# Making the y of two batches together in a fused scan and two MLPs kernel

## The chip, the core and the metric

The kernel runs on one core of a Trainium2 chip. The metric is the device time of one execution in microseconds: 617.73 as the median of three runs (617.5 to 618.22).

## What is computed

A gated linear scan (the mixer) is followed by two MLPs. For each batch b (4), head h (8) and chunk of the sequence, with cum the running sum of log a within the chunk:

```python
L = np.exp(cum[:, :, :, None] - cum[:, :, None, :]) * causal
M = np.einsum('bhin,bhjn->bhij', Cc, Bc) * L
y_intra = np.einsum('bhij,bhjd->bhid', M, xc)
y_inter = np.einsum('bhin,bhnd->bhid', Cc, state) * np.exp(cum)[:, :, :, None]
y[:, :, sl] = y_intra + y_inter
state = decay_full[:, :, None, None] * state + np.sum(Bx, axis=2)
...
x = softplus(x @ w_in) @ w_out        # first MLP, 3072 x 256 -> 2048 -> 256
x = gelu_sigmoid(x @ w2_in) @ w2_out  # second MLP, the same sizes
```

d = 32 columns of x per head, 16 states per head, 3072 = 4 x 768 positions.

## The kernel before

The sequence is cut into NC = 6 chunks of T = 128 positions. A *sub-chunk* s is one batch of one chunk: s = 4c + b, 24 in all. The main loop (line 510) has steps t; step t makes one slice of 128 hidden columns of an MLP for all 512 positions of a chunk (`g1`, six matmuls of 512 columns, line 359) and the second matrix product of the slice of two steps before (`g2`, lines 370 to 377: six matmuls with 512 columns; for t below 18 two matmuls in float32, each in two passes). 16 steps make a chunk. Steps 0 to 95 are the first MLP, 96 to 191 the second.

The mixer runs one chunk ahead of the first MLP, woven into steps 0 to 79: four steps for each sub-chunk, s = (c+1)*4 + (t mod 16)//4, with k = t mod 4 telling the part. Sub-chunks 0 to 3 are done before the loop. The order in each engine's queue is the order of the program text (the schedule is manual), so a function's place in the loop is its place in the queues:

- k = 0: `at_cb(s, 0)` on TensorE (C B^T for four heads, into the single PSUM bank `cb`); `at_small(s)`: two scans of dc on VectorE, cd = dc * ci and bs = B * last column of L on GpSimd.
- k = 1: `at_m(s, 0)` on VectorE (M = cb * L), which frees the bank for `at_cb(s, 1)`; `at_prep(s+1)` (tb, tc on ACT or VectorE, lb and rhs_bd on GpSimd).
- k = 2: `at_m(s, 1)`; `at_y(s)` and `at_u(s)` on TensorE.
- k = 3: `at_out(s)` (ACT copies y to xh, VectorE makes xl), `at_state(s)`, `at_scan(s+1)` (L of the next sub-chunk), `at_load(s+2)` (the loads, all on SP's queue).

`at_y(s)` has first the eight state products, on 32 rows and 32 columns each: head h of a group of four sits at rows 32h of state and cd and writes partitions 32h of y, so these use the four diagonal tiles of the array, twice (line 291). Then come eight products with M, all 128 rows and 32 columns (line 298), and `at_u` has eight more with 32 columns of data for the state's update (line 310). All are float32, two passes each.

In steps 0 to 13 the weights of the first MLP are put together from 64-bit words on VectorE, ACT and GpSimd as well (`w_sign`, `w_join_hi`, `w_join_lo`, `wi_split`; lines 103 to 142); in steps 14 to 28 w1o is split into a high and a low part on ACT and VectorE (`wo_split`).

Of the kernel before, what the change touches and what calls it, by code (L numbers as in the profile page):

```python
# [9 lines left out]
F32 = mybir.dt.float32  # L10
# [16 lines left out]
NT = NC * NF  # L27

PL_B, PL_C, PL_X, PL_BN, PL_W = 0, 128, 256, 512, 640
SP_B, SP_C, SP_X, SP_BN, SP_CI, SP_W = 0, 512, 1024, 1280, 1408, 1664  # L30

HI_SCALE = 2.0**-112


@with_exitstack
def mixer_two_mlps(ctx: ExitStack, tc: tile.TileContext, pack_p, pack_s, a_l, a_rows, consts, w1i, w1o, w2i, w2o, out):
    nc = tc.nc

    wts = ctx.enter_context(tc.tile_pool(name="wts", bufs=1))
# [111 lines left out]

    sub = {}

    def at_load(s):
        at_load_a(s)
        at_load_p(s)

    def at_load_a(s):
        c, b = divmod(s, NB)
        d = sub.setdefault(s, {})  # L160
        d["abz"] = at.tile([P, NH, T], F32, tag="abz", name=f"abz{s}")
        abz = d["abz"].rearrange("p h t -> p (h t)")
        r0 = s * NH
        if s < 2:
            for g in range(2 - s):
                o = slice(g * TB, (g + 1 + s) * TB)
                nc.sync.dma_start(out=abz[:, o], in_=a_l[s : s + 1, o].to_broadcast([P, (1 + s) * TB]))
        else:
            nc.sync.dma_start(
                out=abz, in_=scr_z[r0 : r0 + NH, :].rearrange("(o h) t -> o (h t)", o=1).to_broadcast([P, NH * T])  # L170
            )
        if c > 0:
            d["ad"] = at.tile([P, 2, T], F32, tag="ad", name=f"ad{s}")
            src = scr_a[r0 : r0 + NH, :].rearrange("(g h) t -> h g t", g=2)
            for h in range(4):
                nc.sync.dma_start(out=d["ad"][32 * h : 32 * h + 32], in_=src[h : h + 1].to_broadcast([32, 2, T]))

    def at_load_p(s):
        c, b = divmod(s, NB)
        d = sub.setdefault(s, {})  # L180
        if s < NB:
            pk = x2[:, (0, 1, 4, 5)[s]].rearrange("p k t -> p (k t)")
        else:
            pk = at.tile([P, SP_W], F32, tag="pk", name=f"pk{s}")
        if c == 0:
            nc.sync.dma_start(out=pk[:, 0:PL_W], in_=pack_p[s])
            d["B"], d["C"], d["x"], d["bn"] = pk[:, 0:PL_C], pk[:, PL_C:PL_X], pk[:, PL_X:PL_BN], pk[:, PL_BN:PL_W]
        else:
            nc.sync.dma_start(out=pk, in_=pack_s[s - NB])
            d["B"], d["C"], d["x"] = pk[:, 0:SP_C], pk[:, SP_C:SP_X], pk[:, SP_X:SP_BN]  # L190
            d["bn"], d["ci"] = pk[:, SP_BN:SP_CI], pk[:, SP_CI:SP_W]

    def at_prep(s):
        d = sub[s]
# [30 lines left out]
    def at_scan(s, half=0):  # L225
        d = sub[s]
        if "L" not in d:
            d["L"] = at.tile([P, NH, T], F32, tag="L", name=f"L{s}")
        h = slice(4 * half, 4 * half + 4) if s == 0 else slice(0, NH)
        if s < 2:  # L230
            clip(d["abz"][:, h], d["abz"][:, h])
            nc.vector.memset(d["abz"][:, h, 0:1], 0.0)
        nc.vector.tensor_tensor_scan(  # L233
            out=d["L"][:, h].rearrange("p h t -> p (h t)"), data0=d["abz"][:, h].rearrange("p h t -> p (h t)"),
            data1=eye8[:, h.start * T : h.stop * T], initial=0.0, op0=ALU.mult, op1=ALU.add,
        )

    def at_small(s):
        c, b = divmod(s, NB)
        d = sub[s]  # L240
        if c > 0:
            d["dc"] = at.tile([P, 2, T], F32, tag="dc", name=f"dc{s}")
            for g in range(2):
                nc.vector.tensor_tensor_scan(
                    out=d["dc"][:, g, :], data0=d["ad"][:, g, :], data1=zr, initial=1.0, op0=ALU.mult, op1=ALU.add
                )
            d["cd"] = at.tile([P, 2, T], F32, tag="cd", name=f"cd{s}")
            nc.gpsimd.tensor_tensor(
                out=d["cd"].rearrange("p g t -> p (g t)"), in0=d["dc"].rearrange("p g t -> p (g t)"), in1=d["ci"], op=ALU.mult
            )  # L250
        if c < NC - 1:
            nc.gpsimd.tensor_tensor(
                out=bs_t[s % 2][:, :, 0, :], in0=d["bn"].rearrange("p (h n) -> p h n", h=NH),
                in1=d["L"][:, :, T - 1 : T].to_broadcast([P, NH, N]), op=ALU.mult,
            )

    def at_cb(s, g):
# [14 lines left out]
    def at_m(s, g):  # L272
        d = sub[s]
        if s < NB:
            d["M", g] = hid.tile([P, TB], F32, tag="eg"[g], name=f"M{s}_{g}", bufs=2 + g).rearrange("p (h t) -> p h t", h=4)
        else:
            d["M", g] = at.tile([P, 4, T], F32, tag=f"M{g}", name=f"M{s}_{g}", bufs=1)
        nc.vector.tensor_mul(  # L278
            d["M", g].rearrange("p h t -> p (h t)"), d["cb", g], d["L"][:, 4 * g : 4 * g + 4, :].rearrange("p h t -> p (h t)")
        )  # L280

    def at_y(s):
        c, b = divmod(s, NB)
        d = sub[s]
        y = d["y"] = ps_y.tile([P, 512], F32, tag="y", name=f"y{s}")


        for g in range(2 if c > 0 else 0):
            for h in range(4):
                r = slice(32 * h, 32 * h + 32)  # L290
                nc.tensor.matmul(  # L291
                    y[r, g * T : g * T + T], state[b][r, g, :], d["cd"][r, g, :], start=(g == 0), stop=False,
                    skip_group_check=True,
                )
        for g in range(2):
            for h in range(4):
                x0 = g * P + h * D
                nc.tensor.matmul(  # L298
                    y[32 * h : 32 * h + 32, g * T : g * T + T], d["x"][:, x0 : x0 + D], d["M", g][:, h, :],
                    start=(c == 0), stop=True, skip_group_check=True,  # L300
                )

    def at_u(s):
        d = sub[s]
        y = d["y"]
        if s < NSUB - NB:
            for g in range(2):
                for h in range(4):
                    x0 = g * P + h * D
                    nc.tensor.matmul(  # L310
                        y[32 * h : 32 * h + 32, 256 + g * D : 256 + g * D + D],
                        bs_t[s % 2][:, 4 * g + h].rearrange("p s n -> p (s n)"), d["x"][:, x0 : x0 + D],
                        start=True, stop=True, skip_group_check=True,
                    )
# [29 lines left out]
    def at_pe(s, k):  # L344
        if k < 2:
            at_cb(s, k)
        elif k == 2:
            at_y(s)
            at_u(s)

    tt = {}
# [50 lines left out]
    with tc.manual_schedule():  # L402
# [107 lines left out]
        for t in range(2 * NT + 2):  # L510
# [25 lines left out]
            if mixing and late:  # L536
                at_pe(s, k)

            xl_of = at_out(s) if mixing and k == 3 else None
            if t < 2 * NT:  # L540
                d = tt[t]
                d["g"] = hid.tile([P, TB], F32, tag="g", name=f"g{t}")
# [13 lines left out]
            if t in (1, 3):  # L556
                at_state(2 + t // 2)
            if mixing:
                if k == 0:
                    at_small(s)  # L560
                elif k == 1:
                    if s + 1 < NSUB:
                        at_prep(s + 1)
                elif k == 3:
                    xl_of()
                    at_state(s)
                    if s + 1 < NSUB:
# [53 lines left out]
def _lay_out(x, a, B, C):  # L621
# [4 lines left out]
    xn = xc.transpose(0, 1, 3, 2, 4).reshape(NSUB, T, NH * D)  # L626
    bn = Bc.transpose(0, 1, 3, 2, 4).reshape(NSUB, T, NH * N)
    ci = Cc.reshape(NC, NB, 2, 4, T, N).transpose(0, 1, 3, 5, 2, 4)
    ci = np.broadcast_to(ci[:, :, :, None], (NC, NB, 4, 2, N, 2, T)).reshape(NSUB, P, 2 * T)

    def pairs(v):
        v = v[1:].reshape(NC - 1, NB, 4, 2, T, N).transpose(0, 1, 3, 5, 2, 4)
# [37 lines left out]
```

## Time and profile before

| | |
|---|---|
| median of three runs | 617.73 us (617.5 to 618.22) |
| the profiled execution: its own time | 617.93 us |
| its span, first to last instruction | 616.0 us |
| granted TensorE clock, mean | 0.993 |
| TensorE busy | 589.6 us, 96% of the span |
| VectorE busy | 378.0 us, 61% |
| ACT busy | 292.7 us, 48% |
| GpSimd busy | 158.2 us, 26% |

PE is TensorE's matmul, PEld its weight load, DVE VectorE, POOL GpSimd, SP the queue that issues the transfers. Times in the rows below are in microseconds from the span's start. The start-to-start distance of TensorE's rows tells how fast it goes; the durations overlap, since matmuls are pipelined.

### The profile page before, as it was taken

How to read it: one execution, taken by the hardware profiler on the slowest of the kernel's cores; microseconds unless marked ns; L12 is line 12 of the kernel's file. 1: busy time of each engine (PE TensorE's matmuls, PEld its weight loads, DVE VectorE, ACT ScalarE, POOL GpSimd, SP SyncE). 2: the span in 40 equal slices, each digit the busy share in tenths (PEclk: the TensorE clock that was granted, in tenths of full speed). 3: DMA queues.
4: the chain of work that ended last, by engine and by line, in shares of the span. 5: the costliest groups of instructions: out<-in, count | busy, mean ns of one | idle time of the engine just before them, and what ended most of it. 6: DMA issues, size and time to landing. Idle time of an engine off the chain costs nothing.

```text
span 616.0 us, 8790 instructions
## 1 busy us (share of the span) xinstructions
PE 589.6 (96%) x3392; PEld 461.2 (75%) x3392; DVE 378.0 (61%) x526; ACT 292.7 (48%) x501; POOL 158.2 (26%) x135
## 2 busy tenths in 40 slices
PE   4788889999999999999999999999999999999997
PEld 1355546888788888777788887888888888888885
DVE  5999996998877777787377699323323332332221
ACT  3344434454443444434455777544544554554543
POOL 2655444544454344453021233100000000000000
PEclk9889999999999999999999999999999999999999
DMA  6857653434334243343022241000000000000000
GB/s 209 279 194 234 214 196 106 147 100 138 102 99 147 107 141 99 99 139 118 2 69 77 94 145 61 35 1 0 35 0 1 34 2 0 35 1 0 35 0 34
DMA packets 24408, 54.39 MB, mean 88 GB/s; under 512 B 2832, under 2 KB 8368, under 8 KB 24368
## 3 DMA queue, kind: packets, MB, share of 16 engines
q1 hardware_dynamic: 24368, 53.85, 26.2%
q8 instruction: 26, 0.43, 0.3%
q14 instruction: 14, 0.11, 0.1%
HBM read 50.50 MB, written 3.34 MB: 87 GB/s over the span
## 4 chain that ended last, share of the span: by engine, by line
PE 81%; DVE 9%; DMA 3%; issue 3%; SPq 1%; POOL 1%; ACT 1%; DVEq 0%
PE h L359 37%; PE o L375 13%; PE o L377 12%; PE o L376 12%; PE y L298 2%; PE y L291 1%; DVE L L233 1%; PE cb L267 1%; DVE x L132 1%; DMA ac<-a_rows 1%; DMA pk<-pack_s 1%; DVE wt_1o L127 1%; DVE wt_1i L127 1%; PE o L373 1%; DMA wraw_1i<-w1i 1%
## 5 line engine op out<-in xcount | busy, mean ns | idle before, releaser
L76 DVE TENSOR_TENSOR gl<-g,gh 128x512 fp32r<-128x512 f32 x176 | 141.6, 806 | 170.1 <-ACT gh L382 170.0
L543 ACT ACTIVATE g<-h 128x512 f32<-128x512 f32 x192 | 114.8, 598 | 253.5 <-PE h L359 248.2
L382 ACT ACTIVATE gh<-g 128x512 fp32r<-128x512 f32 x176 | 111.3, 632 | 5.6
L359 PE MATMUL h<-xh,w1ih 128*128 128x512 f32 x192 | 78.6, 409 | 0.5 <-ACT xh L326 0.5
L359 PE MATMUL h<-xl,w1ih 128*128 128x512 f32 x192 | 76.2, 397 | 0.0
L377 PE MATMUL o<-gl,w2oh 128*128 128x512 f32 x192 | 74.8, 390 | 0.2 <-DVE gl L76 0.2
L359 PE MATMUL h<-x2h,w2ih 128*128 128x512 f32 x192 | 74.7, 389 | 0.0
L375 PE MATMUL o<-gh,w2ol 128*128 128x512 f32 x192 | 74.7, 389 | 0.0
L376 PE MATMUL o<-gh,w2oh 128*128 128x512 f32 x192 | 74.7, 389 | 0.0
L359 PE MATMUL h<-x2l,w2ih 128*128 128x512 f32 x192 | 74.7, 389 | 0.0
L79 POOL TENSOR_TENSOR rhs_bd<-tc,pk 64x512 fp32r<-64x512 f32 x40 | 65.1, 1628 | 1.5
L375 PE MATMUL o<-gh,w1ol 128*128 128x512 f32 x160 | 64.3, 402 | 0.0
L359 PE MATMUL h<-xh,w1il 128*128 128x512 f32 x192 | 60.2, 395 | 3.9 <-POOL w1il L79 3.9
L376 PE MATMUL o<-gh,w1oh 128*128 128x512 f32 x160 | 62.4, 390 | 0.0
L377 PE MATMUL o<-gl,w1oh 128*128 128x512 f32 x160 | 62.4, 390 | 0.0
L233 DVE TENSOR_TENSOR_SCAN L<-abz,eye 128x1024 f32<-128x1024 f32 (+1 forms) x25 | 61.8, 2474 | 0.2
L359 PE MATMUL h<-x2h,w2il 128*128 128x512 f32 x192 | 59.1, 389 | 0.0
L278 DVE TENSOR_TENSOR M<-cb,L 128x512 f32<-128x512 f32 x48 | 32.7, 686 | 28.3 <-PE cb L267 28.2
L359 PEld LDWEIGHTS h<-xh,w1il 128*128 128x128 f32 x192 | 36.2, 190 | 13.7 <-POOL w1il L79 5.6
L359 PEld LDWEIGHTS h<-xh,w1ih 128*128 128x128 f32 x192 | 36.6, 191 | 8.1 <-ACT xh L326 1.0
L377 PEld LDWEIGHTS o<-gl,w2oh 128*128 128x128 f32 x192 | 36.0, 188 | 8.2 <-DVE gl L76 0.7
L359 PEld LDWEIGHTS h<-xl,w1ih 128*128 128x128 f32 x192 | 36.6, 190 | 7.0 <-issue 1.0
(96 smaller groups left out, 753.0 us busy)
## 6 DMA issues: line engine op xcount, KB each, us to landing
pk<-pack_s SPq DMA_DIRECT2D x20, 832.0 KB, 4.6
abz<-scr_z SPq DMA_DIRECT2D x22, 512.0 KB, 3.7
wraw_1i<-w1i SPq DMA_DIRECT2D x8, 512.0 KB, 4.5
wraw_1o<-w1o SPq DMA_DIRECT2D x8, 512.0 KB, 3.6
wraw_2i<-w2i SPq DMA_DIRECT2D x8, 512.0 KB, 3.7
wraw_2o<-w2o SPq DMA_DIRECT2D x8, 512.0 KB, 3.4
out<-ot SPq DMA_DIRECT2D x12, 256.0 KB, 2.0
ad<-scr_a SPq DMA_DIRECT2D x80, 32.0 KB, 2.5
```

The lines of the kernel that those rows point to most:

```text
L76: nc.vector.tensor_sub(o, x, y)
L79: nc.gpsimd.tensor_tensor(out=o, in0=x, in1=y, op=ALU.subtract)
L127: nc.vector.scalar_tensor_tensor(out=tu, in0=tu, scalar=3, in1=s, op0=ALU.logical_shift_left, op1=ALU.bitwise_or)
L233: nc.vector.tensor_tensor_scan(out=d["L"][:, h].rearrange("p h t -> p (h t)"), data0=d["abz"][:, h].rearrange("p h t -> p (h t)"), data1=e ...
L278: nc.vector.tensor_mul(d["M", g].rearrange("p h t -> p (h t)"), d["cb", g], d["L"][:, 4 * g : 4 * g + 4, :].rearrange("p h t -> p (h t)"))
L298: nc.tensor.matmul(y[32 * h : 32 * h + 32, g * T : g * T + T], d["x"][:, x0 : x0 + D], d["M", g][:, h, :], start=(c == 0), stop=True, skip ...
L359: nc.tensor.matmul(h, w[:, k, f], x[:, k, :], start=(n == 0), stop=(n == 5))
L375: nc.tensor.matmul(acc[c][j], wl[:, m, o], d["gh"], start=first, stop=False)
L376: nc.tensor.matmul(acc[c][j], wh[:, m, o], d["gh"], start=False, stop=False)
L377: nc.tensor.matmul(acc[c][j], wh[:, m, o], d["gl"], start=False, stop=last)
L382: nc.scalar.activation(d["gh"], d["g"], AF.Copy)
L543: nc.scalar.activation(d["g"], d["h"], AF.Softplus if t < NT else AF.Gelu_apprx_sigmoid)
```

## The change

`at_y` and `at_u` of an even and the following odd sub-chunk are issued together, at k = 2 of the odd one. The odd sub-chunk keeps its state, ad, dc, cd and ci turned by 32 partitions (`rows(s, h)`: head h at rows 32((h+1) mod 4)), and its u is written there; its y stays at partitions 32h. The 16 state products of the two alternate between the sub-chunks, so that eight consecutive products have eight different tiles, and the two y are in two PSUM banks. M is written over L instead of into a tile of its own, L has three buffers; because bs reads L's last column, `at_small` makes bs first, and stands ahead of `at_m(s, 0)` in step 0. x, bn and ci are a transfer of their own (px, three buffers), and pk keeps B and C. At k = 3 of an odd sub-chunk both xh are copied, both xl made, then the next L, then both states.

```diff
-SP_B, SP_C, SP_X, SP_BN, SP_CI, SP_W = 0, 512, 1024, 1280, 1408, 1664
+SP_B, SP_C, SP_W = 0, 512, 1024
+SX_X, SX_BN, SX_CI, SX_W = 0, 256, 384, 640
...
+    def rows(s, h):
+        r = 32 * ((h + s % 2) % 4)
+        return slice(r, r + 32)
...
-                nc.sync.dma_start(out=d["ad"][32 * h : 32 * h + 32], in_=src[h : h + 1].to_broadcast([32, 2, T]))
+                nc.sync.dma_start(out=d["ad"][rows(s, h)], in_=src[h : h + 1].to_broadcast([32, 2, T]))
...
+            pk = at.tile([P, SP_W], F32, tag="pk", name=f"pk{s}")
+            px = at.tile([P, SX_W], F32, tag="px", name=f"px{s}", bufs=3)
             nc.sync.dma_start(out=pk, in_=pack_s[s - NB])
-            d["B"], d["C"], d["x"] = pk[:, 0:SP_C], pk[:, SP_C:SP_X], pk[:, SP_X:SP_BN]
-            d["bn"], d["ci"] = pk[:, SP_BN:SP_CI], pk[:, SP_CI:SP_W]
+            nc.sync.dma_start(out=px, in_=pack_x[s - NB])
+            d["B"], d["C"] = pk[:, 0:SP_C], pk[:, SP_C:SP_W]
+            d["x"], d["bn"], d["ci"] = px[:, 0:SX_BN], px[:, SX_BN:SX_CI], px[:, SX_CI:SX_W]
...
-            d["L"] = at.tile([P, NH, T], F32, tag="L", name=f"L{s}")
+            d["L"] = at.tile([P, NH, T], F32, tag="L", name=f"L{s}", bufs=3)
...
     def at_small(s):
         c, b = divmod(s, NB)
         d = sub[s]
+        if c < NC - 1:
+            nc.gpsimd.tensor_tensor(
+                out=bs_t[s % 2][:, :, 0, :], in0=d["bn"].rearrange("p (h n) -> p h n", h=NH),
+                in1=d["L"][:, :, T - 1 : T].to_broadcast([P, NH, N]), op=ALU.mult,
+            )
         if c > 0:
             d["dc"] = at.tile([P, 2, T], F32, tag="dc", name=f"dc{s}")
...
-        if c < NC - 1:
-            nc.gpsimd.tensor_tensor(
-                out=bs_t[s % 2][:, :, 0, :], in0=d["bn"].rearrange("p (h n) -> p h n", h=NH),
-                in1=d["L"][:, :, T - 1 : T].to_broadcast([P, NH, N]), op=ALU.mult,
-            )
...
-            d["M", g] = at.tile([P, 4, T], F32, tag=f"M{g}", name=f"M{s}_{g}", bufs=1)
+            d["M", g] = d["L"][:, 4 * g : 4 * g + 4, :]
...
+    def at_y(*ss):
+        for s in ss:
+            sub[s]["y"] = ps_y.tile([P, 512], F32, tag="y", name=f"y{s}")
+
+
+        for g in range(2 if ss[0] >= NB else 0):
             for h in range(4):
...
+                for s in ss:
+                    d, r = sub[s], rows(s, h)
+                    nc.tensor.matmul(
+                        d["y"][32 * h : 32 * h + 32, g * T : g * T + T], state[s % NB][r, g, :], d["cd"][r, g, :],
+                        start=(g == 0), stop=False, skip_group_check=True,
+                    )
+        for s in ss:
+            d = sub[s]
+            for g in range(2):
+                for h in range(4):
+                    x0 = g * P + h * D
+                    nc.tensor.matmul(
+                        d["y"][32 * h : 32 * h + 32, g * T : g * T + T], d["x"][:, x0 : x0 + D], d["M", g][:, h, :],
+                        start=(s < NB), stop=True, skip_group_check=True,
+                    )
...
-        elif k == 2:
-            at_y(s)
+        elif k == 2 and s % 2:
+            at_y(s - 1, s)
+            at_u(s - 1)
             at_u(s)
...
-            xl_of = at_out(s) if mixing and k == 3 else None
+            xl_of = [at_out(i) for i in (s - 1, s)] if mixing and k == 3 and s % 2 else []
...
             if t == 0:
+                at_small(s)
                 at_m(s, 0)
...
-                if k == 0:
+                if k == 0 and t > 0:
                     at_small(s)
...
-                    xl_of()
-                    at_state(s)
+                    for f in xl_of:
+                        f()
                     if s + 1 < NSUB:
                         at_scan(s + 1)
+                    for i in (s - 1, s) if s % 2 else ():
+                        at_state(i)
```

The host's layout follows: ci of odd batches is rolled by one group of 32 partitions, and pack_s is cut into pack_s and pack_x.

## Rows read from the trace of the kernel before

**Rows 1.** The page: shares of the engines, and the chain by engine.

```profile
PE 589.6 (96%) x3392; PEld 461.2 (75%) x3392; DVE 378.0 (61%) x526; ACT 292.7 (48%) x501; POOL 158.2 (26%) x135
...
PE 81%; DVE 9%; DMA 3%; issue 3%; SPq 1%; POOL 1%; ACT 1%; DVEq 0%
```

**Rows 2.** Stages: stretch, length, each engine's busy time (instructions), granted clock, DMA.

```profile
28.83:96.31 67.48, 59.01 (x376) 35.39 (x377) 63.53 (x83) 28.20 (x49) 35.82 (x29) 0.96 0.62 209
110.37:149.15 38.78, 38.78 (x302) 31.30 (x300) 37.90 (x51) 19.06 (x34) 18.61 (x15) 1.00 0.35 118
149.15:303.87 154.72, 154.72 (x1138) 124.06 (x1136) 114.14 (x161) 64.82 (x112) 62.85 (x53) 1.00 0.33 109
```

**Rows 3.** TensorE's timeline, steps 58 to 60: start, length, instruction, count.

```profile
232.67 0.40 PE L359 MATMUL h<-xh,w1ih 128*128 128x512 f32 x1
...
234.16 0.64 PE L291 MATMUL y<-cd,st 32*32 32x128 f32 x16
234.73 0.64 PE L298 MATMUL y<-M,pk 128*32 128x128 f32 x16
235.19 0.31 PE L310 MATMUL y<-pk,bs 128*32 128x32 f32 x16
235.43 0.50 PE L375 MATMUL o<-gh,w1ol 128*128 128x512 f32 x1
235.76 0.40 PE L376 MATMUL o<-gh,w1oh 128*128 128x512 f32 x1
236.00 0.39 PE L377 MATMUL o<-gl,w1oh 128*128 128x512 f32 x1
...
236.92 0.39 PE L359 MATMUL h<-xh,w1ih 128*128 128x512 f32 x1
...
239.64 0.39 PE L359 MATMUL h<-xh,w1ih 128*128 128x512 f32 x1
```

**Rows 4.** TensorE's timeline, starts of steps 78 and 79.

```profile
297.01 0.40 PE L359 MATMUL h<-xh,w1ih 128*128 128x512 f32 x1
...
301.13 0.40 PE L359 MATMUL h<-xh,w1ih 128*128 128x512 f32 x1
```

**Rows 5.** Line 291 alone in step 78: PE, PEld busy (passes begun by then).

```profile
298.45:298.60 0.15, 0.11 (x4) 0.11 (x8) 1.00 0.00 0
...
298.45:298.80 0.35, 0.31 (x12) 0.31 (x16) 1.00 0.00 0
```

**Rows 6.** ACT's timeline in step 9; in brackets the idle time before.

```profile
72.38 0.72 ACT L199 ACTIVATE tb<-pk,cc 128x512 fp32r<-128x512 f32 x1 [0.90 <-DMA pk<-pack_s]
```

**Rows 7.** Timelines of GpSimd, VectorE and TensorE in steps 12 to 14.

```profile
86.47 1.09 POOL L248 TENSOR_TENSOR cd<-dc,pk 128x256 f32<-128x256 f32 x1 [7.22 <-DVE dc L244]
87.52 0.41 POOL L252 TENSOR_TENSOR bs<-pk,L 128x128 f32<-128x128 f32 x1
...
92.29 0.68 DVE L278 TENSOR_TENSOR M<-cb,L 128x512 f32<-128x512 f32 x1
...
93.03 0.43 PE L298 MATMUL y<-M,pk 128*32 128x128 f32 x8 [0.24 <-DVE M L278]
```

**Rows 8.** Timeline of steps 18 to 20: GpSimd and VectorE.

```profile
105.94 3.44 POOL L79 TENSOR_TENSOR rhs_bd<-tc,pk 64x512 fp32r<-64x512 f32 x2
...
106.46 1.77 DVE L76 TENSOR_TENSOR w1ol<-x,w1oh 128x512 fp32r<-128x512 f32 x1
...
109.86 0.41 DVE L76 TENSOR_TENSOR xl<-y,xh 128x256 fp32r<-128x256 f32 x1
...
110.50 2.28 DVE L233 TENSOR_TENSOR_SCAN L<-abz,eye 128x1024 f32<-128x1024 f32 x1
...
113.29 0.68 DVE L76 TENSOR_TENSOR w1ol<-x,w1oh 128x512 fp32r<-128x512 f32 x1
```

**Rows 9.** Timeline of step 21: M and the cb that takes its bank.

```profile
114.54 0.67 DVE L278 TENSOR_TENSOR M<-cb,L 128x512 f32<-128x512 f32 x1
...
116.10 0.40 PE L267 MATMUL cb<-rhs_bd,lb 128*128 128x256 f32 x2
```

More of the change, by code (lines that the diff above doesn't have):

```diff
@@ L29, with mixer_two_mlps @@
 PL_B, PL_C, PL_X, PL_BN, PL_W = 0, 128, 256, 512, 640
-SP_B, SP_C, SP_X, SP_BN, SP_CI, SP_W = 0, 512, 1024, 1280, 1408, 1664
+SP_B, SP_C, SP_W = 0, 512, 1024
+SX_X, SX_BN, SX_CI, SX_W = 0, 256, 384, 640
 HI_SCALE = 2.0**-112
 @with_exitstack
-def mixer_two_mlps(ctx: ExitStack, tc: tile.TileContext, pack_p, pack_s, a_l, a_rows, consts, w1i, w1o, w2i, w2o, out):
+def mixer_two_mlps(ctx: ExitStack, tc: tile.TileContext, pack_p, pack_s, pack_x, a_l, a_rows, consts, w1i, w1o, w2i, w2o, out):
     nc = tc.nc
@@ L180, in at_load_p @@
         d = sub.setdefault(s, {})
-        if s < NB:
+        if c == 0:
             pk = x2[:, (0, 1, 4, 5)[s]].rearrange("p k t -> p (k t)")
-        else:
-            pk = at.tile([P, SP_W], F32, tag="pk", name=f"pk{s}")
-        if c == 0:
             nc.sync.dma_start(out=pk[:, 0:PL_W], in_=pack_p[s])
@@ L280, in at_m @@
         )
[L282 to L288, printed above, removed]
-            for h in range(4):
[L290 to L301, printed above, removed]
+    def at_y(*ss):
+        for s in ss:
+            sub[s]["y"] = ps_y.tile([P, 512], F32, tag="y", name=f"y{s}")
+        for g in range(2 if ss[0] >= NB else 0):
+            for h in range(4):
+                for s in ss:
[13 more added lines that the diff above has]
+                    )
     def at_u(s):
         d = sub[s]
-        y = d["y"]
         if s < NSUB - NB:
@@ L310, in at_u @@
                     nc.tensor.matmul(
-                        y[32 * h : 32 * h + 32, 256 + g * D : 256 + g * D + D],
+                        d["y"][rows(s, h), 256 + g * D : 256 + g * D + D],
                         bs_t[s % 2][:, 4 * g + h].rearrange("p s n -> p (s n)"), d["x"][:, x0 : x0 + D],
@@ L628, in _lay_out @@
     ci = Cc.reshape(NC, NB, 2, 4, T, N).transpose(0, 1, 3, 5, 2, 4)
-    ci = np.broadcast_to(ci[:, :, :, None], (NC, NB, 4, 2, N, 2, T)).reshape(NSUB, P, 2 * T)
+    ci = np.broadcast_to(ci[:, :, :, None], (NC, NB, 4, 2, N, 2, T)).copy()
+    ci[:, 1::2] = np.roll(ci[:, 1::2], 1, axis=2)
+    ci = ci.reshape(NSUB, P, 2 * T)
     def pairs(v):
@@ L639, in _lay_out @@
     pack_p = np.concatenate([first(Bc), first(Cc), xn[:NB], bn[:NB]], axis=2)
-    pack_s = np.concatenate([pairs(Bc), pairs(Cc), xn[NB:], bn[NB:], ci[NB:]], axis=2)
+    pack_s = np.concatenate([pairs(Bc), pairs(Cc)], axis=2)
+    pack_x = np.concatenate([xn[NB:], bn[NB:], ci[NB:]], axis=2)
     a_l = a.reshape(NB, NH, NC, T).transpose(2, 0, 1, 3)
-    return pack_p, pack_s, a_l.reshape(NSUB, NH * T), a_l.reshape(NSUB * NH, T)
+    return pack_p, pack_s, pack_x, a_l.reshape(NSUB, NH * T), a_l.reshape(NSUB * NH, T)
 def _consts():
@@ L655 @@
     from concourse.bass_utils import run_bass_kernel_spmd
-    pack_p, pack_s, a_l, a_rows = _lay_out(x, a, B, C)
-    arrays = {"pack_p": pack_p, "pack_s": pack_s, "a_l": a_l, "a_rows": a_rows, "consts": _consts()}
+    pack_p, pack_s, pack_x, a_l, a_rows = _lay_out(x, a, B, C)
+    arrays = {"pack_p": pack_p, "pack_s": pack_s, "pack_x": pack_x, "a_l": a_l, "a_rows": a_rows, "consts": _consts()}
     arrays = {k: np.ascontiguousarray(v) for k, v in arrays.items()}
```

## The prediction

> **What bounds the kernel now.** I read the page first, for the engines' shares and the chain that ended last; then the stages, for where TensorE has idle time; then the timeline of one step that holds a y; then what ends the idle time of the first 16 steps. The reader is to see that TensorE is busy for 96% of the span and carries 81% of the chain that ended last [rows 1]. By stage: in the first 16 steps (28.83 to 96.31) TensorE is busy 59.0 of 67.5 us and VectorE 63.5, so VectorE and what feeds it set the pace there. From 110.37 on TensorE is busy in every microsecond up to 303.87 [rows 2]. There a microsecond taken from TensorE's queue is a microsecond of the kernel, as long as nothing else becomes late. VectorE is nearly full in one more place, 110.37 to 149.15 (steps 20 to 31), where it has 0.9 us of idle time in 38.8 [rows 2].
>
> **What a y costs on TensorE.** A step begins with its first L359. Step 58 (k = 2, with a y) runs from 232.67 to 236.92, 4.25 us; step 59 without one from 236.92 to 239.64, 2.72 [rows 3]. The y and u of one sub-chunk thus cost 1.52 us. In the last mixing chunk, without u, step 78 takes 301.13 - 297.01 = 4.12 us [rows 4], a cost of 1.40; so u is 0.12.
>
> The 1.52 splits up like this. A sub-chunk has 8 state products, each a matmul in two passes: 16 records. By 298.60 four passes have started, by 298.80 twelve [rows 5]: they go in rounds of four, one on each of the four tiles on the diagonal, about 0.11 us a round, four rounds, 0.44 us. The products with M also are 16 records of 128 columns on four tiles, and u starts 235.19 - 234.73 = 0.46 us after them [rows 3]: again 0.44. What is left, 1.52 - 0.44 - 0.44 - 0.12 = 0.52 us, is the price of changing the tile shape three times (128x128 to 32x32 to 128x32 to 128x128). It shows at each border: L298 starts 0.57 after L291 where four rounds are 0.44, and the first L375 after the y takes 0.33 to the next start where the next take 0.24 [rows 3].
>
> **The change on TensorE.** The eight sub-chunk pairs of steps 16 to 79 lie in the stretch that TensorE bounds. A pair before: 2 x 1.52 = 3.04 us. After: one set of shape changes, 0.52; 32 passes of state products on eight tiles, which I put at four rounds of eight, 0.44 + 0.03 (starts within a round are spread wider); products with M for two, 0.88; u for two, 0.24. Sum 2.11, a saving of 0.93. Without u: 2.80 - 1.87 = 0.93 as well. Eight pairs: 7.4 us. Half of the 0.93 is the shape changes (0.52), the other half the rounds (0.41).
>
> The rounds are the uncertain half. That four 32x32 tiles with different rows and columns run together is in the trace, and that four 128x32 tiles that share all rows and differ in columns do, too. Two tiles in the same columns at once is not: the even sub-chunk's product sits at rows 32h, the odd one's at rows 32(h+1), both end in columns 32h. The bounds are four rounds (eight at once) and eight rounds (four at once), 0.44 us apart for a pair. I take four, because the nearest rows, the products with M, show tiles that share all their rows running together at the full round of 0.11 us, and because the two y go to two banks. [...] No row of this trace has two row tiles in one column.
>
> **What moves on the other engines.** ACT copies two xh in the odd k = 3 step instead of one in each; ACT is busy less than half of these stages [rows 2], so nothing. VectorE's xl and state updates of the even sub-chunk (together 0.65 us, from xl's start to the scan's [rows 8]) move four steps later, and the state updates behind the scan. At a chunk's end two xl stand before the next g1 instead of one, but the y they need is issued in the step before, as it was, and one xl of 0.41 us [rows 8] is covered by the g2 of that step (six starts 0.24 apart). M written over L takes as many elements as before. It adds one wait: the write of M must come after GpSimd has read the last column of L for bs. That is why bs goes first in at_small. GpSimd stood idle 7.2 us before cd in step 12 [rows 7], so bs runs in that idle time; behind the waiting M stand gl and the next cb, which show no lateness as long as bs is done before M's own cb. Without that cover it would cost bs's 0.41 us [rows 7] per sub-chunk. pk as two transfers: 20 more issues on SP, in front of nothing but later loads, for buffers that come free a step or more ahead (px has three, since x of the even sub-chunk lives longer). Nothing for these after step 16.
>
> **Steps 0 to 15.** TensorE's saving is not on the path there. Four things are. (a) VectorE must reach M of sub-chunk 7 (92.29), and TensorE waits for it 0.24 us [rows 7]; xl and the state updates of sub-chunk 6 were before it and now come after: 0.65 us earlier. (b) in step 9 ACT stood 0.90 us idle until pk of sub-chunk 7 had landed [rows 6]; with B and C alone it is 512 of 832 KB, so part of the 0.90 should go, and all of it is the most. (c) In step 14 the pair is 2.11 - 1.52 = 0.59 us longer than the single y was, less the 0.24 of waiting that the even sub-chunk's products now fill: 0.35 lost. (d) In step 0 the two dc scans and bs now go ahead of M: M is later by them, and GpSimd's queue (cd, then w1il, for which TensorE waits in step 2) is earlier by the M and the join that it stood behind; I count the two as even, a few tenths either way. The bounds are a gain of 2.0 (a, all of b, and d at 0.4) and a loss of 0.6 (neither a nor b counts, c stays, d costs 0.3). I take a gain of 0.7: a, 0.4 of b, less c.
>
> **Steps 16 to 31.** VectorE and GpSimd get in each other's way: w1ol took 1.77 us behind a rhs_bd and 0.68 without [rows 8]. TensorE gets faster by 1.86 over the two pairs of steps 16 to 31; VectorE had 0.9 us idle in most of that stretch [rows 2]. The tightest place I found is step 21: M ended at 115.21, the cb that needs its bank started at 116.10 [rows 9], 0.9 us of room; TensorE will come 1.52 earlier (no y in step 18) and VectorE 0.65. That just fits. Bounds 0 and 1.86 - 0.9 = 1.0; I take 0.2.
>
> Sum: 7.4 + 0.7 - 0.2 = 7.9 us less than the profiled execution's 617.93, which is 0.2 above the median of 617.73: 609.8. Its own range: 7.4 + 2.0 gives 608.3, 7.4 - 0.6 - 1.0 gives 611.9.
>
> **Rivals.**
> 1. Four at a time: two tiles in the same columns do not run together, or the engine doesn't look far enough ahead in its queue. Eight rounds, the pair takes 0.52 + 0.88 + 0.88 + 0.24 = 2.52, saving 0.52; 8 x 0.52 + 0.5 = 4.7 us, 613.0. For it: no row shows more than four at once. Against: each tile has its own rows and bank here.
> 2. VectorE takes over in steps 16 to 31 and nothing is gained up to there: six pairs are left, 5.6 us, 612.1. For it: VectorE's 0.9 us of idle time in 38.8. Against: the room in [rows 9], and 114.1 of 154.7 us busy from 149.15 on [rows 2].
> 3. Slower: the passes go in program order. In the program the two passes of one product follow each other on one tile, so in strict order each product's second pass waits out the first, and the next product starts with it: 17 rounds, a pair of 0.52 + 1.87 + 0.88 + 0.24 = 3.51 us, 0.47 more than before, 8 x 0.47 - 0.5 = 3.3 us, 621.0. It decides from 12.7 rounds on (3.04 - 0.52 - 0.88 - 0.24 = 1.40, by 0.11). Against it: strict order would give nine rounds, 0.99 us, for the eight products of before, and they take 0.57 with the shape change; so passes of other tiles overtake a waiting one. Whether they overtake when seven wait instead of three, and across tiles of one column, no row shows. [...]
> 4. No change to speak of: a new wait (M for bs, or the odd y for its cd) costs what the pairs save, 0.93 us for each of the eight. The idle 7.2 us on GpSimd speaks against it.
>
> **How the numbers follow.** The forecast has 0.62, rival 1 0.18, rival 2 0.08, rival 3 0.07, rival 4 0.05. The time is the forecast's, 609.8. The range takes the forecast's own lower end, 608.2, and goes up past rivals 1 and 2 to 613.5; rivals 3 and 4 and some of rival 1's tail are left out. About 0.2% (1.2 us) is what a measurement of this kernel can tell from no change. Faster by more than that: 0.62 + 0.18 + 0.08, and a little of rival 4: 0.89; same 0.04; slower 0.07.
>
> **What the profile after would show.** Steps of k = 2: even ones at 2.72 us, odd ones at 4.83 (2.72 + 2.11); with rival 1 at 5.24, with rival 3 at 6.2. By 0.15 us after the first state product eight passes should have started, not four. L298 should start about 0.6 us after L291. Steps 0 to 15 should end near 95.6 instead of 96.31. No idle time on TensorE between 110 and 300; idle before cb, ended by M, would be rival 2; idle before M, ended by bs, rival 4. I would be wrong above all if tiles in one column exclude each other.

## The result, and the profile after

The changed kernel takes 610.31 us (609.87 to 610.39) where the kernel before took 617.62 on the same chip: a ratio of 0.9879 (95% interval in brackets: [0.9862, 0.9896]). The forecast was 609.8. The profiled execution took 610.23 us, its span is 608.5.

The page after, the rows that answer to [rows 1]; TensorE's busy time is 6.9 us less for the same number of instructions:

```profile
PE 582.7 (96%) x3392; PEld 457.7 (75%) x3392; DVE 381.7 (63%) x526; ACT 292.3 (48%) x501; POOL 158.8 (26%) x135
...
PE 79%; DVE 10%; DMA 4%; issue 2%; POOL 2%; ACT 1%; SPq 0%; DVEq 0%; ACTq 0%; POOLq 0%
```

The stages that answer to [rows 2] (steps 0 to 15, 20 to 31, 32 to the end of the mixing; columns as there):

```profile
28.66:95.62 66.96, 59.01 (x376) 34.70 (x377) 63.49 (x79) 27.93 (x49) 35.89 (x29) 0.94 0.64 218
108.17:147.12 38.95, 38.86 (x349) 31.54 (x348) 38.91 (x49) 19.22 (x35) 18.62 (x16) 1.00 0.38 118
147.12:296.64 149.52, 149.52 (x1137) 122.39 (x1136) 117.92 (x165) 64.60 (x112) 64.57 (x53) 1.00 0.35 113
```

In steps 20 to 31 VectorE now has 0.04 us of idle time (38.91 of 38.95) and TensorE 0.09; from 147.12 on TensorE is the bound, as before.

TensorE's timeline after. First the odd step with the pair (step 54) and the start of steps 55 and 56; then an even step without a y (58), with the cb ahead of it; then steps 78 and 79, the pair without u. These rows answer to [rows 3, 4]:

```profile
214.58 0.40 PE L369 MATMUL h<-xh,w1ih 128*128 128x512 f32 x1
...
216.06 0.67 PE L299 MATMUL y<-cd,st 32*32 32x128 f32 x32
216.66 1.08 PE L308 MATMUL y<-L,px 128*32 128x128 f32 x32
217.56 0.48 PE L319 MATMUL y<-px,bs 128*32 128x32 f32 x32
217.96 0.50 PE L385 MATMUL o<-gh,w1ol 128*128 128x512 f32 x1
...
219.46 0.39 PE L369 MATMUL h<-xh,w1ih 128*128 128x512 f32 x1
...
222.18 0.39 PE L369 MATMUL h<-xh,w1ih 128*128 128x512 f32 x1
...
227.91 0.40 PE L274 MATMUL cb<-rhs_bd,lb 128*128 128x256 f32 x2
228.14 0.40 PE L369 MATMUL h<-xh,w1ih 128*128 128x512 f32 x1
...
230.91 0.39 PE L369 MATMUL h<-xh,w1ih 128*128 128x512 f32 x1
...
289.34 0.40 PE L369 MATMUL h<-xh,w1ih 128*128 128x512 f32 x1
...
293.92 0.39 PE L369 MATMUL h<-xh,w1ih 128*128 128x512 f32 x1
```

Step 54 is 219.46 - 214.58 = 4.88 us, step 58 is 2.77; the two were 4.25 each [rows 3]. The 32 passes of state products take 0.60 us to the next line's start, hardly more than the 0.57 that 16 took before. The pair without u makes step 78 4.58 us long.

The state products' line alone in step 78 (PE and PEld busy, in brackets the passes begun by then); it answers to [rows 5]:

```profile
290.78:290.93 0.15, 0.11 (x8) 0.11 (x16) 1.00 0.00 0
...
290.78:291.13 0.35, 0.31 (x24) 0.31 (x32) 1.00 0.00 0
```

Eight passes have begun by 0.15 us and 24 by 0.35, where it was four and twelve: eight tiles run together, in rounds of the same 0.11 us.

The lengths of the stretches, worked out from the starts of their first L359 (L369 after), give the account:

| steps | before, us | after, us | difference | predicted |
|---|---|---|---|---|
| start of step 0 | 28.83 | 28.66 | -0.17 | 0 |
| 0 to 15 | 67.48 | 66.96 | -0.52 | -0.7 |
| 16 to 31 (two pairs) | 52.84 | 51.50 | -1.34 | -1.66 |
| 32 to 63 (four pairs) | 103.41 | 100.08 | -3.33 | -3.72 |
| 64 to 79 (two pairs, no u) | 51.31 | 49.44 | -1.87 | -1.86 |
| 80 to the end | 312.18 | 311.81 | -0.37 | 0 |
| span | 616.05 | 608.45 | -7.60 | -7.9 |

Two rows of it are not the change's. The start of step 0 lay anywhere from 27.6 to 29.1 in the twelve executions profiled, and steps 80 to the end, which the change does not touch, took 311.78 to 312.18. I could not attribute either. Kernels that differ by a few tenths are therefore compared below by their stretches, not by their totals.

From step 16 on, one step without a pair got longer by more than 0.03 us: step 21, 3.36 us instead of 3.01. The timelines of VectorE, TensorE and GpSimd after, in step 14 (which answers to [rows 7]) and in steps 20 and 21 (to [rows 9]); in brackets the idle time before and its releaser:

```profile
91.06 0.86 PE L308 MATMUL y<-L,px 128*32 128x128 f32 x24
91.43 0.68 DVE L285 TENSOR_TENSOR L<-cb,L 128x512 f32<-128x512 f32 x1
92.16 0.43 PE L308 MATMUL y<-L,px 128*32 128x128 f32 x8 [0.24 <-DVE L L285]
...
111.37 0.66 DVE L77 TENSOR_TENSOR gl<-g,gh 128x512 fp32r<-128x512 f32 x1
111.58 0.72 POOL L249 TENSOR_TENSOR bs<-px,L 128x128 f32<-128x128 f32 x1 [2.88 <-issue]
111.96 0.90 DVE L77 TENSOR_TENSOR w1ol<-x,w1oh 128x512 fp32r<-128x512 f32 x1
113.43 0.66 DVE L285 TENSOR_TENSOR L<-cb,L 128x512 f32<-128x512 f32 x1
114.14 0.30 PEld L274 LDWEIGHTS cb<-rhs_bd,lb 128*128 128x128 f32 x2 [0.51 <-DVE L L285]
```

TensorE's weight load for the second cb stands idle 0.51 us until M has freed the bank. In front of that M, w1ol and bs ran into each other: bs, begun while gl ran, took 0.72 us instead of the 0.41 of step 12 [rows 7], and w1ol 0.90 instead of 0.68 [rows 8].

### The profile page after: what moved, and what is told of

It reads as the page before. It is cut to its first block, busy times and chain, and to the rows that moved or that the text cites. A ratio compares the mean times of both kernels' runs of the same rounds, so it can differ in the third digit from the quotient of the medians.

```text
span 608.5 us, 8823 instructions
## 1 busy us (share of the span) xinstructions
PE 582.7 (96%) x3392; PEld 457.7 (75%) x3392; DVE 381.7 (63%) x526; ACT 292.3 (48%) x501; POOL 158.8 (26%) x135
## 3 DMA queue, kind: packets, MB, share of 16 engines
HBM read 50.50 MB, written 3.34 MB: 88 GB/s over the span
## 4 chain that ended last, share of the span: by engine, by line
PE 79%; DVE 10%; DMA 4%; issue 2%; POOL 2%; ACT 1%; SPq 0%; DVEq 0%; ACTq 0%; POOLq 0%
PE h L369 37%; PE o L385 12%; PE o L387 12%; PE o L386 12%; DVE L L240 2%; DMA ad<-scr_a 2%; PE y L308 1%; PE cb L274 1%; DMA ac<-a_rows 1%; POOL rhs_bd L80 1%; DVE gl L77 1%; PE o L383 1%; PE y L299 1%; DVE x L133 1%; DVE wt_1i L128 1%
## 5 line engine op out<-in xcount | busy, mean ns | idle before, releaser
L369 PE MATMUL h<-xh,w1ih 128*128 128x512 f32 x192 | 79.0, 411 | 0.5 <-ACT xh L335 0.5
L369 PE MATMUL h<-xl,w1ih 128*128 128x512 f32 x192 | 75.9, 395 | 0.0
L369 PE MATMUL h<-x2h,w2ih 128*128 128x512 f32 x192 | 74.7, 389 | 0.0
L369 PE MATMUL h<-x2l,w2ih 128*128 128x512 f32 x192 | 74.7, 389 | 0.0
L240 DVE TENSOR_TENSOR_SCAN L<-abz,eye 128x1024 f32<-128x1024 f32 (+1 forms) x25 | 64.4, 2575 | 0.2
L369 PE MATMUL h<-xh,w1il 128*128 128x512 f32 x192 | 60.3, 395 | 2.3 <-POOL w1il L80 2.3
L369 PE MATMUL h<-x2h,w2il 128*128 128x512 f32 x192 | 59.1, 389 | 0.0
L369 PEld LDWEIGHTS h<-xh,w1il 128*128 128x128 f32 x192 | 35.9, 189 | 11.9 <-POOL w1il L80 4.1
L369 PEld LDWEIGHTS h<-xh,w1ih 128*128 128x128 f32 x192 | 36.8, 191 | 8.4 <-ACT xh L335 1.2
L369 PEld LDWEIGHTS h<-xl,w1ih 128*128 128x128 f32 x192 | 36.5, 190 | 7.5 <-issue 1.4
L386 PEld LDWEIGHTS o<-gh,w2oh 128*128 128x128 f32 x192 | 36.0, 188 | 7.5
```

The lines of the kernel that those rows point to most:

```text
L240: nc.vector.tensor_tensor_scan(out=d["L"][:, h].rearrange("p h t -> p (h t)"), data0=d["abz"][:, h].rearrange("p h t -> p (h t)"), data1=e ...
L369: nc.tensor.matmul(h, w[:, k, f], x[:, k, :], start=(n == 0), stop=(n == 5))
L386: nc.tensor.matmul(acc[c][j], wh[:, m, o], d["gh"], start=False, stop=False)
```

## The experiments

Each is the changed kernel with the edit shown.

**The odd sub-chunk on the same tiles as the even one.** The pair stays, the turn by 32 partitions goes (on the host the roll of ci goes with it), so sixteen products share four tiles.

```diff
     def rows(s, h):
-        r = 32 * ((h + s % 2) % 4)
+        r = 32 * h
```

> The pair as changed, but the odd sub-chunk is not turned: its state products use the same four diagonal tiles as the even one's. My theory (half of a pair's gain is that eight passes go at once, half is the shape changes shared): the state products of a pair take eight rounds instead of four, 0.44 us more for each of the eight pairs of steps 16 to 79, odd k = 2 steps of 5.32 us (4.88 before that edit) and 5.02 without u; 3.5 us more than the change, about 613.8. Rival (the gain is all shape changes, the rounds are hidden behind something else): no difference, 610.3.

Measured: 613.85 us (613.4 to 613.98), ratio 0.9939 [0.9925, 0.9954]. The state products' line alone, and TensorE's timeline of step 54:

```profile
217.73:217.88 0.15, 0.11 (x4) 0.11 (x8) 1.00 0.70 137
217.73:218.08 0.35, 0.31 (x12) 0.31 (x16) 1.00 0.51 105
```

```profile
216.29 0.40 PE L369 MATMUL h<-xh,w1ih 128*128 128x512 f32 x1
...
217.77 1.11 PE L299 MATMUL y<-cd,st 32*32 32x128 f32 x32
218.81 1.08 PE L308 MATMUL y<-L,px 128*32 128x128 f32 x32
221.62 0.39 PE L369 MATMUL h<-xh,w1ih 128*128 128x512 f32 x1
```

Four passes by 0.15 us and twelve by 0.35: four at a time, eight rounds. L299 takes 1.04 us instead of 0.60, the step 5.33 instead of 4.88. Over eight pairs that is 3.6 us, and the totals differ by 3.5. Pairing without the turn gives half of the gain, the turn the other half, as the prediction split it.

**The odd sub-chunk's products behind the even one's.** Same sixteen products on the same eight tiles, but the even sub-chunk's eight first, so that products for the other four tiles stand 32 instructions (16 weight loads, 16 passes) behind.

```diff
         for g in range(2 if ss[0] >= NB else 0):
             for h in range(4):
                 for s in ss:
...
+        for s in ss:
+            for g in range(2 if s >= NB else 0):
+                for h in range(4):
```

> The pair on eight tiles, but all eight state products of the even sub-chunk stand ahead of the odd one's in the program. Theory A (an instruction is held up by a waiting one ahead of it beyond some reach, so the order of the products matters): eight rounds, odd k = 2 steps of 5.3 us, about 613.8. Theory B (whatever tile is free takes its next pass, whatever stands ahead): four rounds, 4.88 us, 610.3. In between if the odd one's passes come in before the even one's are through.

Measured: 609.99 us (609.34 to 611.42), ratio 0.9881 [0.9865, 0.9898]; steps 32 to 63 take 100.19 us (100.08 in the change). The products' line alone in step 54, and TensorE's timeline there:

```profile
215.10:215.18 0.08, 0.04 (x4) 0.04 (x7) 1.00 0.81 102
215.10:215.25 0.15, 0.11 (x8) 0.12 (x16) 1.00 0.43 55
```

```profile
215.14 0.69 PE L299 MATMUL y<-cd,st 32*32 32x128 f32 x32
215.76 1.08 PE L308 MATMUL y<-L,px 128*32 128x128 f32 x32
```

Eight passes have again begun by 0.15 us: first four, within 0.04 us of the first of all (215.14), then four more, within 0.11 of it. The trace does not name the tile of a pass. That the second four are the odd sub-chunk's follows from the kernels where the passes share four tiles: in the experiment before this one the fifth pass had not begun 0.11 us after the first (217.77), and in the kernel before, it began 0.13 after the first (298.49 and 298.62 in step 78). So they began ahead of the even one's waiting passes. The odd step takes 4.91 us instead of 4.88: the order in which the change writes the products is worth 0.03 us a pair, the tiles 0.45. Passes for free tiles thus started ahead of earlier ones whose tile was busy, four of them within 0.11 us of the first of all.

**The pairs undone, everything else of the change kept** (turned rows, bs first, M over L, px by itself).

```diff
-        elif k == 2 and s % 2:
-            at_y(s - 1, s)
-            at_u(s - 1)
+        elif k == 2:
+            at_y(s)
             at_u(s)
...
-            xl_of = [at_out(i) for i in (s - 1, s)] if mixing and k == 3 and s % 2 else []
+            xl_of = [at_out(s)] if mixing and k == 3 else []
...
-                    for i in (s - 1, s) if s % 2 else ():
-                        at_state(i)
+                    at_state(s)
```

> Everything of the change but the pairing: each sub-chunk makes its y and u in its own k = 2 step again, xl and the state updates are in every k = 3 step; M over L, bs first, px and the turned odd sub-chunk stay. My theory (the time comes from the pairing, the rest is worth a few tenths in steps 0 to 15 at most): k = 2 steps of 4.24 us as before, 617.2. Rival (M over L, bs first and the split transfer are worth a microsecond or more by themselves, either way): 616 or less, or 618.5 or more.

Measured: 617.68 us against 617.51 for the kernel before, ratio 1.0 [0.999, 1.001]. Its steps 0 to 15 as a stage, the start and the end of step 58 on TensorE, ACT in step 9 (which answers to [rows 6]) and VectorE's M of sub-chunk 7 (to [rows 7]):

```profile
28.50:96.12 67.62, 58.72 (x376) 34.80 (x377) 63.98 (x81) 27.56 (x49) 35.37 (x29) 0.97 0.64 215
```

```profile
232.47 0.40 PE L368 MATMUL h<-xh,w1ih 128*128 128x512 f32 x1
...
236.72 0.39 PE L368 MATMUL h<-xh,w1ih 128*128 128x512 f32 x1
```

```profile
71.95 0.72 ACT L206 ACTIVATE tb<-pk,cc 128x512 fp32r<-128x512 f32 x1 [0.53 <-DMA pk<-pack_s]
...
92.10 0.68 DVE L285 TENSOR_TENSOR L<-cb,L 128x512 f32<-128x512 f32 x1
```

The step is 4.25 us again, and steps 0 to 15 are back at 67.62. So the whole gain is the pairing's, that of the first 16 steps too; pk in two transfers, M over L and the new order in step 0, taken together, give nothing without it. ACT's wait for pk is shorter (0.53 us, 0.90 in [rows 6]), yet M of sub-chunk 7 begins 63.60 us after step 0, as late as before the change (63.46).

**One small product in the even steps.** One 32x32x32 product stands in each even k = 2 step from step 18 on, which brings back two changes of the tile shape; the pair later overwrites its result.

```diff
-            sub[s]["y"] = ps_y.tile([P, 512], F32, tag="y", name=f"y{s}")
+            if "y" not in sub[s]:
+                sub[s]["y"] = ps_y.tile([P, 512], F32, tag="y", name=f"y{s}")
...
+        elif k == 2 and s % 2 == 0 and s >= 2 * NB:
+            y = sub[s]["y"] = ps_y.tile([P, 512], F32, tag="y", name=f"y{s}")
+            nc.tensor.matmul(
+                y[0:32, 0:32], state[s % NB][0:32, 0, :], sub[s]["cd"][0:32, 0, 0:32], start=True, stop=True,
+                skip_group_check=True,
+            )
```

> The change, with one 32x32 state product of 32 columns added in each even k = 2 step from step 18 on (8 in all; what it writes is overwritten), so that the array changes shape and back there without a y. My theory (a change of shape costs some 0.17 us, three of them 0.52): two changes, 0.35 us, and 0.1 for the product's two passes, even k = 2 steps of 3.2 us instead of 2.77; 8 x 0.45 = 3.6 us more, about 613.9. Rival (the shape change costs next to nothing, the 0.52 us are the fill of each group of products): at most 0.1 us a step, 611.1 or less.

Measured: 613.15 us (611.82 to 615.18), ratio 0.9932 [0.991, 0.9954]. TensorE's timeline of step 58:

```profile
230.90 0.40 PE L376 MATMUL h<-xh,w1ih 128*128 128x512 f32 x1
...
232.38 0.24 PE L359 MATMUL y<-cd,st 32*32 32x32 f32 x2
232.56 0.50 PE L392 MATMUL o<-gh,w1ol 128*128 128x512 f32 x1
232.89 0.40 PE L393 MATMUL o<-gh,w1oh 128*128 128x512 f32 x1
...
234.05 0.39 PE L376 MATMUL h<-xh,w1ih 128*128 128x512 f32 x1
```

The even step is 3.15 us instead of 2.77: 0.38 for one product with 32 columns of data. In it are two changes of shape and two passes, where the prediction puts 0.52 for three changes. Eight of them are 3.0 us. Step 21 is back at 3.01 us in this kernel, where TensorE comes to it 0.4 us later, so steps 16 to 79 are 2.65 us longer than in the change. The totals differ by 2.8, but the four executions here lie 3.4 us apart, and the profiled one, 615.18, is 1.2 us longer in step 14 alone, at a lower granted clock (last section).

A rival to the shape is the number type, since the small products are float32 in two passes and the full-size matmuls around them are not. The trace of the kernel before tells the two apart, as its g2 is float32 at full size (L373, passes 0.43 us apart) in steps 10 and 11:

```profile
73.31 1.88 PE L373 MATMUL o<-g,x 128*128 128x512 f32 x4
75.11 0.64 PE L291 MATMUL y<-cd,st 32*32 32x128 f32 x16
...
77.42 0.62 PE L359 MATMUL h<-xh,w1il 128*128 128x512 f32 x2
77.88 1.88 PE L373 MATMUL o<-g,x 128*128 128x512 f32 x4
```

From g1's last two matmuls to the float32 passes it is 0.46 us, two starts of 0.23: the new type costs nothing here. From four float32 passes to the small float32 products it is 1.80 us, 0.09 more than four times 0.43: the new shape does cost. So going to a small tile and back is dear here, 0.38 us with one product computed there, and this is the other half of what pairing saves: 0.83 a pair, less the turn's 0.45, is 0.38.

**M in tiles of its own** (as before the change, now two per half; L with two buffers).

```diff
-            d["L"] = at.tile([P, NH, T], F32, tag="L", name=f"L{s}", bufs=3)
+            d["L"] = at.tile([P, NH, T], F32, tag="L", name=f"L{s}", bufs=2)
...
-            d["M", g] = d["L"][:, 4 * g : 4 * g + 4, :]
+            d["M", g] = at.tile([P, 4, T], F32, tag=f"M{g}", name=f"M{s}_{g}", bufs=2)
```

> The change with M in tiles of its own again (two buffers each, L two), bs still first. My theory (M over L costs and gives nothing, the write's wait for bs is hidden): the same step times as the change, 2.77 and 4.88 us, 610.3. Rival (the wait of M for bs shows, most likely in steps 0 to 15 or in the late cb of step 21, 3.36 us instead of 3.01): step 21 or the start of step 16 earlier by 0.2 us or more.

Measured: 610.16 us against 618.51 for the kernel before, ratio 0.9868 [0.9853, 0.9883]. Every stretch is the change's within 0.1 us (66.91, 51.49, 100.08, 49.44), step 21 is 3.36. The wait of M for bs costs nothing; M over L saves memory beside this kernel (three tiles of L instead of two and four half tiles of M), not time.

**bs behind cd again**, on the kernel with M in its own tiles, where nothing asks for bs first; at_small is back behind at_m in step 0.

```diff
     def at_small(s):
-        if c < NC - 1:
-            nc.gpsimd.tensor_tensor(
-                out=bs_t[s % 2][:, :, 0, :], in0=d["bn"].rearrange("p (h n) -> p h n", h=NH),
-                in1=d["L"][:, :, T - 1 : T].to_broadcast([P, NH, N]), op=ALU.mult,
-            )
         if c > 0:
...
+        if c < NC - 1:
+            nc.gpsimd.tensor_tensor(
+                out=bs_t[s % 2][:, :, 0, :], in0=d["bn"].rearrange("p (h n) -> p h n", h=NH),
+                in1=d["L"][:, :, T - 1 : T].to_broadcast([P, NH, N]), op=ALU.mult,
+            )
```

> As the kernel with M in its own tiles, and bs behind cd again, and at_small behind M in step 0, as before the change. My theory (bs first meets VectorE's w1ol, which took 0.90 us beside it in step 20 instead of 0.68, and so makes M of sub-chunk 9 and the cb of step 21 late): step 21 falls from 3.36 to about 3.15 us, nothing else moves from step 16 on; steps 0 to 15 within 0.4 us either way; 610.1. Rival (bs first is what makes steps 0 to 15 shorter): step 16 starts 0.5 us later than in the change, 610.6.

Measured: 609.47 us, ratio 0.9864 [0.9846, 0.9881]. VectorE ahead of step 21's cb:

```profile
111.46 0.68 DVE L77 TENSOR_TENSOR w1ol<-x,w1oh 128x512 fp32r<-128x512 f32 x1
112.71 0.66 DVE L285 TENSOR_TENSOR M<-cb,L 128x512 f32<-128x512 f32 x1
```

w1ol is back at 0.68 us, step 21 at 3.14 instead of 3.36, steps 16 to 31 at 51.28 (51.50). So 0.22 of step 21's 0.35 came from bs in front of cd. Steps 0 to 15 are 66.94, beside 66.91 with bs first: the order within step 0 makes no difference.

**w1o's split one step later**, so that w1ol does not fall into step 20.

```diff
-            if NF - 2 <= t < 2 * NF - 2 and m % 2 == 0:
-                q = (t - NF + 2) // 2
+            if NF - 1 <= t < 2 * NF - 1 and m % 2 == 1:
+                q = (t - NF + 1) // 2
```

> The change with the split of w1o (on ACT and, two steps later, VectorE) one step later each, so that no w1ol stands before M of sub-chunk 9 in VectorE's queue. My theory (VectorE's queue makes M of sub-chunk 9 late for the cb in step 21): step 21 takes 3.01 instead of 3.36 us, 609.95. Rival (the split is then late for its g2): waits before line 385 in steps 20 to 33, 610.3 or more.

Measured: 610.27 us, ratio 0.9872 [0.9857, 0.9887]. Step 21 is 3.01, but step 20 is 3.34. VectorE and TensorE's weight load there:

```profile
107.99 1.77 DVE L77 TENSOR_TENSOR w1ol<-x,w1oh 128x512 fp32r<-128x512 f32 x1
109.82 0.19 PEld L385 LDWEIGHTS o<-gh,w1ol 128*128 128x128 f32 x1 [0.52 <-DVE w1ol L77]
```

w1ol now meets a rhs_bd, takes 1.77 us, and is itself what TensorE waits for. The lateness moved by a step, at the same price or a little more: steps 16 to 31 take 51.64 us (51.50).

**tb and tc on ACT for sub-chunks 8 to 11**, which takes two operations from VectorE in each.

```diff
-            if s < 2 * NB:
+            if s < 3 * NB:
                 nc.scalar.activation(o, i, AF.Identity, scale=mask)
```

> The change with tb and tc of sub-chunks 8 to 11 on ACT instead of VectorE (0.9 us less for VectorE, 1.4 us more for ACT, each sub-chunk). My theory as for the later split: step 21 takes 3.01 us, 609.95. Rival (ACT becomes late with gh, or rhs_bd with tc): idle time on TensorE in steps 16 to 31 that the change doesn't have.

Measured: 609.6 us, ratio 0.9866 [0.9847, 0.9885]; step 21 is 3.16, steps 16 to 31 are 51.28. Less work for VectorE gives back 0.2 us of the 0.35.

**The two together** (bs behind cd, tb and tc on ACT, M in its own tiles), and the change once more beside it.

```diff
-            if s < 2 * NB:
+            if s < 3 * NB:
...
-            d["M", g] = d["L"][:, 4 * g : 4 * g + 4, :]
+            d["M", g] = at.tile([P, 4, T], F32, tag=f"M{g}", name=f"M{s}_{g}", bufs=2)
...
     def at_small(s):
-        if c < NC - 1:
...
+        if c < NC - 1:
...
```

> The change with M in its own tiles, bs behind cd as before the change, and tb and tc of sub-chunks 8 to 11 on ACT: the two edits that each took 0.2 of the 0.35 us of lateness out of step 21. My theory (both shorten VectorE's queue ahead of M of sub-chunk 9): step 21 at 3.01 us, steps 16 to 31 in 51.15 us where the change takes 51.50, the whole 0.35 us below the change, 609.95, which a comparison of the totals can hardly tell. Rival (step 21 waits for something else beyond 0.2 us): step 21 stays at 3.14.

> The changed kernel as it is, on the same chip as the one before, for the comparison: 610.3, step 21 at 3.36 us, steps 16 to 31 in 51.50 us; the start of step 0 may differ by some tenths from run to run.

Measured: 610.7 us (609.23 to 612.2), ratio 0.988 [0.9859, 0.9902], beside 610.47 (609.55 to 610.77), ratio 0.9874 [0.9857, 0.989], for the change. Steps 16 to 31 of the two together as a stage:

```profile
96.11:147.26 51.15, 51.15 (x399) 40.53 (x398) 46.20 (x59) 28.66 (x51) 25.53 (x20) 1.00 0.37 119
```

Step 21 is 3.01 again and the stage 0.34 us shorter than the change's beside it (51.49, with TensorE busy for 51.41), and TensorE is busy throughout. In the total this can't be seen: step 0 began 0.55 us later in this kernel's profiled execution (29.13 against 28.58), within what it varies by anyway. No version here is measurably better than the change.

## Why the prediction was right

**The mechanism and the rounds: right.** Eight tiles run together in four rounds; rival 1 is excluded by the rows of step 78, and the kernel with the same tiles shows what it would have been, at 613.85 where rival 1 was put at 613.0. Rival 3 (program order) would have made odd steps 6.2 us; they are 4.88, and with the odd sub-chunk's products behind the even one's 4.91. One argument for the rounds, that the two y go to two banks, is borne out by no run, and against rival 1 it is not right that each tile has its own bank. The four state products of one sub-chunk sit on four row tiles and all write the bank of its y, each its own partitions, in the kernel before too, and there they ran four at a time [rows 5]. Whether two tiles in one column need two banks is not shown, since the two y had two banks in every run.

**The pair: 0.93 put, 0.83 measured with u.** 2 x 4.243 - (4.884 + 2.770) = 0.83, with one more digit of the trace than the rows show. Two terms were mis-sized by 0.05 to 0.06 each. The first is the 1.52 for "the y and u of one sub-chunk", taken as the difference of step 58 to step 59. Without a y, step 58 is 2.77, not 2.72: a cb stands ahead of it, and the matmuls that follow a cb start up to 0.24 us apart for a while instead of 0.23. So 0.05 of the 1.52 was never y's, and stays in the even step. The second is u: with the two u, step 54 is 0.30 longer than step 78 (4.88 and 4.58), where 0.24 was put. Without u the pair makes the odd step 4.58 - 2.72 = 1.86 longer, against 1.87 put. In steps 64 to 79 each pair gained 0.93 as put, but by luck: the k = 2 steps give 0.89, the 0.05 of the cb being missed here too, and the k = 3 steps, which the prediction left out, give 0.04, since step 79 takes 2.72 us after and took 303.87 - 301.13 = 2.74 before [rows 2, 4]. Six pairs with u at 0.83 and two at 0.93 make 6.9 instead of 7.4.

**The split into halves: right in the main.** The turn is worth 0.45 per pair by the kernel without it (0.41 put). The rest, 0.38, is the visit to the small tiles that a pair saves (0.52 put), and one visit with a single product cost 0.38 as well.

**Steps 0 to 15: 0.52 instead of 0.7, and its terms differ.** (a) held: counted from step 0, the M of sub-chunk 7 begins 63.46 us in before [rows 7] and 62.77 after, 0.69 earlier (0.65 put), and without pairs it is back at 63.60. (b), 0.4 for the smaller pk, gave nothing: without pairs, but with pk in two transfers, ACT waits 0.37 us less for pk and the steps are no shorter than before. (c) cost 0.17, not 0.35: from that M to step 16 it was 4.02 us and is 4.19, since most of what the pair adds stands ahead of M, where VectorE sets the pace. The 0.24 us of waiting for M was not filled, as I had thought, but stayed: VectorE came earlier, and TensorE too. (d) was even, by the two kernels with M in its own tiles (66.91 and 66.94). So the errors in (b) and (c) partly cancel, and the sum is nearer than its terms.

**Steps 16 to 31: a stall of 0.35 instead of 0.2, at the place named.** The prediction says that step 21 "just fits"; the cb came 0.35 late. The statement that failed is that bs, run in GpSimd's idle time, costs nothing after step 16: in step 20 it falls between VectorE's gl and w1ol and holds up w1ol, and with it M. The rows of the change can be read as a strict sequence, in which gl ends near 111.96 (w1ol's start), bs then runs to 111.58 + 0.72 = 112.30, and w1ol finishes 0.56 later, at 112.86. The kernel with the split moved looks alike: there the rhs_bd beside w1ol ended at 109.22 and w1ol 0.54 later. What holds the two engines up there, no run shows. With bs out of the way 0.22 of the 0.35 went; with tb and tc on ACT 0.20; with both, all of it. Rival 2 thus took place to the extent of one step. Rival 4 did not: M in a tile of its own, which has no need to wait for bs, is as fast.

The sum of the terms as measured is 6.9 + 0.52 - 0.35 = 7.1, and the four stretches give 0.52 + 1.34 + 3.33 + 1.87 = 7.06. The rest up to the 7.6 of the profiled spans lies at the start of step 0 and behind step 80, where the change has no part; that the spans come nearer to the forecast 7.9 than these terms do is luck. The medians differ by 7.3.

## What to carry to other kernels

Where small matmuls stand between full ones, count first how often the tile shape changes, and gather the small ones of several batches into one visit: a visit cost 0.38 us here even for one product. Then give each batch tiles of its own (another row group for operands that would share one), worth 0.45 us a pair here, and, as here, its own PSUM bank (no run tried one bank for both); the order in which they are written mattered little, 0.03 us a pair. And price a step by the same step without the part in question, not by its neighbour.

## What the runs showed of the hardware that was not expected

- With the odd sub-chunk's products behind the even one's, TensorE began four passes for free tiles within 0.11 us of the first pass of all, although the even one's eight products, 32 instructions, stand ahead of them and only four of those 16 passes had begun.
- Two 32x32 tiles in the same columns, with different rows and banks, ran together at the full round of 0.11 us for one pass of 128 float32 columns (the change, step 78).
- Changes of tile shape cost time on TensorE, 0.38 us for a visit of one small product (the kernel with the small product, step 58); a change to float32 at full size cost none (two starts in 0.46 us, the kernel before, step 11).
- In step 58, behind a cb, the twelve full-size matmuls take 2.77 us, in step 59 they take 2.72: 0.004 us more for each. Why is open.
- In the profiled execution of the kernel with the small product, the granted clock was 0.75 in mean over one step, after TensorE had waited 1.72 us for M; the step took 6.85 us where the changed kernel took 5.63. The changed kernel waits 1.72 us at that place too, and its clock stayed at 1.00. What decides is open. The wait and step 14 as a stage, first in the kernel with the small product, then in the changed kernel:

```profile
86.86 0.50 PE L274 MATMUL cb<-rhs_bd,lb 128*128 128x256 f32 x2 [1.72 <-DVE L L285]
```

```profile
87.20:94.05 6.85, 6.85 (x108) 3.86 (x106) 4.89 (x6) 0.83 (x3) 5.19 (x4) 0.75 0.44 151
```

```profile
86.84 0.50 PE L274 MATMUL cb<-rhs_bd,lb 128*128 128x256 f32 x2 [1.72 <-DVE L L285]
```

```profile
87.18:92.81 5.63, 5.39 (x108) 3.22 (x106) 4.89 (x6) 0.82 (x3) 4.01 (x4) 1.00 0.54 189
```
